# Cutting the first wq transfer by partitions: 16 rows, then 112 rows

## The chip, the cores and the metric

The kernel runs on one core of one Trainium2 chip. The metric is the device time of one execution in microseconds (us), lower is better. Beside timed runs there is one execution recorded by the hardware profiler; all places in time below count from the start of its span.

## What is computed

Two independent problems, A and B, of the same shape: one decoding step of sliding-window attention with grouped heads. Each takes two sequences of one token.

```python
def ref(x, k_cache, v_cache, wq, wo):          # x: [2, 1, 576]
    Hq, Dh, Hkv, Sk = 32, 128, 16, 16384
    W = 4096                                   # the window: the last 4096 positions
    q = (x @ wq).reshape(B, 1, Hq, Dh).transpose(0, 2, 1, 3)
    k = repeat(k_cache[:, :, Sk - W:, :], 2, axis=1)
    v = repeat(v_cache[:, :, Sk - W:, :], 2, axis=1)
    p = softmax(einsum("bhqd,bhkd->bhqk", q, k) * Dh ** -0.5)
    o = einsum("bhqk,bhkd->bhqd", p, v)
    return o.transpose(0, 2, 1, 3).reshape(B, 1, Hq * Dh) @ wo
out = concatenate([ref(A), ref(B)], axis=-1)   # bfloat16
```

All inputs are bfloat16. wq is 576 x 4096 (4608 KB), wo is 4096 x 576 (4608 KB), and the windows of K and V are 32 MB each for each problem.

## The kernel before

**Data.** Each problem's K and V are cut into slabs of 4 MB (one sequence, four K/V heads, 4096 positions), eight of K and eight of V for each problem. A slab fills one of four slots of `ring`, 128 partitions by 32,768 bytes. Ahead of the slabs the same memory holds wq: `ringf` is `ring` seen flat, and problem P's wq takes `QW` = 18,432 elements (36,864 bytes) of each partition from `P * QW` on. wq is read as one flat run of memory, cut into 128 equal rows, one for each partition. With 9 groups of 2048 columns in each row it is the right-hand side of the q matmuls.

**Order of the work.** A static list (`_Sched`) holds the operations of each engine in the order in which they were written; for each dependency between engines a semaphore wait is put in front of the operation. A DMA adds 16 to its semaphore when it has landed; `dma_op` takes the number of DMAs that one entry issues, so that a user waits for 16 times that number.

**The DMA queue.** SP issues all large transfers, in this order: wq of A, wq of B (L187), then the slabs (L378) with the parts of wo (L362) between them, and last the output (L658). The four x transfers, two rows each, are issued by ACT (L179). The two wq transfers and the first K slab (slot 3, which wq doesn't reach) wait for nothing. The second K slab goes into slot 0 and waits for the q matmuls of A (`first_deps`); the slabs for slots 1 and 2 wait for those of B. Every later slab waits for the last reader of its slot: the DVE transposes of a K slab (L433) or the PE matmuls of a V slab (L536). The last V slab and the last quarter of wo come in three pieces each (`v_cuts`, `w_cuts`).

**The start.** GpSimd makes constants and masks; DVE spreads and transposes x (L222, L229). PE then runs the q matmuls of A, nine groups of four (L279 for the first of each group, the helper line L264 for the others), as soon as wq of A has landed, and those of B when wq of B has. ACT evacuates q; two small PE steps and GpSimd bring it into the form `zq`.

**The loop.** For each of the 16 K slabs DVE transposes two halves into `xt` (L433), PE multiplies them with `zq` into scores (L459 and L264), and for every two slabs there is a maximum, an exponential on ACT (L497), a transpose on DVE (L506) and the sums. Three slabs later PE multiplies with V (L536), DVE reduces (L559, L566), and the result meets wo (L618, L639).

Of the kernel before, what the change touches and what calls it, by code (L numbers as in the profile page):

```python
# [62 lines left out]
def build_kernel(nc, probs, out):  # L63
# [25 lines left out]
    QW = NU * UW  # L89
# [3 lines left out]
    with es:  # L93
# [50 lines left out]
        ringf = ring[:].rearrange("p r f -> p (r f)")  # L144
# [16 lines left out]
        wq_sem = [sem("wq%d" % P) for P in range(NPROB)]  # L161
# [7 lines left out]
        def dma_op(eng, sem_h, n_dmas, fn, deps, tag):  # L169
            op = S.add(eng, fn, deps, tag)  # L170
            dma_count[sem_h] = dma_count.get(sem_h, 0) + 16 * n_dmas
            op.dma = (sem_h, dma_count[sem_h])
            return op
# [7 lines left out]
            x_dma.append(dma_op("act", x_sem[P], 2, f_x, [], "x%d" % P))  # L181

        wq_dma = {}
        for P in range(NPROB):
            def f_wq(e, P=P):
                src = probs[P][3].rearrange("a b -> (a b)").rearrange("(p f) -> p f", p=128)
                return e.dma_start(ringf[:, P * QW:(P + 1) * QW], src).then_inc(wq_sem[P], 16)  # L187
            wq_dma[P] = dma_op("sp", wq_sem[P], 1, f_wq, [], "wq%d" % P)

        pool = lambda fn, deps, tag: S.add("pool", fn, deps, tag)  # L190
        dve = lambda fn, deps, tag: S.add("dve", fn, deps, tag)
# [600 lines left out]
def bass_concat_heads__sliding_block_cached__sliding_block_cached__decode_kernel(  # L792
    nc, A_x, A_k_cache, A_v_cache, A_wq, A_wo, B_x, B_k_cache, B_v_cache, B_wq, B_wo, out,
):
    build_kernel(nc, [(A_x, A_k_cache, A_v_cache, A_wq, A_wo), (B_x, B_k_cache, B_v_cache, B_wq, B_wo)], out)
# [28 lines left out]
```

## Time and profile before

| | |
|---|---|
| median of 3 runs | 363.3 us (363.21 to 363.47) |
| span of the profiled execution | 361.8 us; its own time is not listed apart from it, the median is 1.5 us longer |
| busy: PE, DVE, ACT, POOL | 240.2, 218.7, 46.0, 24.3 us |
| DMA | 153.26 MB, mean 424 GB/s |
| wq of A: issue on SP, from issue to landing | at 0.80 us, 13.3 us |
| wq of B: issue on SP, from issue to landing | at 1.25 us, 23.8 us |

Busy time is the sum of an engine's instructions in the profiled execution. The time from issue to landing of a transfer holds its wait behind the transfers that were issued before it. The page cuts the span into 40 equal slices of some 9 us; its DMA row gives the mean busy share of the 16 DMA engines in tenths, and the GB/s row what they moved. A timeline row has the start, the duration, the engine, the line of the kernel, the operation with its output and inputs, and in brackets how long the engine had been idle and what released it.

### The profile page before, as it was taken

The numbers are of one execution on the slowest core, as the hardware profiler recorded it, in microseconds if no ns is written. First come the engines' busy times: TensorE is split into PE (matmuls) and PEld (weight loads), VectorE is DVE, ScalarE is ACT, GpSimd is POOL, SyncE is SP. The second block draws the span as 40 slices with busy tenths as digits, with TensorE's granted clock in tenths as the row PEclk, the third lists the DMA queues.
The fourth block names the chain that finished last, engine by engine and source line by source line (L and its number), as shares of the span: only waits on it lengthen the run. The fifth ranks groups of instructions, "written<-read, shape, count | busy, mean of one in ns | idle before, by whom it ended". The sixth has DMA issues, their size and how long they took to land.

```text
span 361.8 us, 2625 instructions
## 1 busy us (share of the span) xinstructions
PE 240.2 (66%) x1292; PEld 57.2 (16%) x927; DVE 218.7 (60%) x150; ACT 46.0 (13%) x78; POOL 24.3 (7%) x84
## 2 busy tenths in 40 slices
PE   0497787666485747662596675567776875668695
PEld 0000111112111201111121121112112121112222
DVE  1901898495929591934909585682927776674622
ACT  1002100040023000500005000500005000500500
POOL 4200101100010001000010000100010001000000
PEclk9999698969988996888788796888688796868969
DMA  8999999999999999999999999999999999999996
GB/s 327 457 435 406 460 408 446 424 431 438 417 453 408 457 404 428 444 431 431 435 420 444 417 449 410 440 431 438 424 442 412 449 417 429 435 435 431 417 412 256
DMA packets 6227, 153.26 MB, mean 424 GB/s; under 512 B 700, under 2 KB 840, under 8 KB 1224
## 3 DMA queue, kind: packets, MB, share of 16 engines
q1 hardware_dynamic: 6196, 153.10, 98.7%
q8 instruction: 8, 0.13, 0.1%
q14 instruction: 3, 0.02, 0.0%
q10 hardware_dynamic: 20, 0.01, 0.0%
HBM read 153.10 MB, written 0.00 MB: 423 GB/s over the span
## 4 chain that ended last, share of the span: by engine, by line
DMA 48%; DVE 26%; PE 16%; issue 8%; ACT 1%; POOL 0%; SPq 0%
DMA ring<-in_B_k_cache_dram 17%; DVE xt L433 16%; DMA ring<-in_A_k_cache_dram 13%; DMA ring<-in_B_v_cache_dram 9%; DMA ring<-in_B_wq_dram 7%; PE st L264 5%; PE st L459 5%; DMA wob<-in_B_wo_dram 3%; PE pj L264 2%; DVE oR L566 2%; DVE mx L467 2%; DVE pT L506 2%; DVE tmp L559 2%; PE ot L536 2%; PE pj L618 1%
## 5 line engine op out<-in xcount | busy, mean ns | idle before, releaser
L459 PE MATMUL st<-xt,zq 128*128 128x512 bf16 x256 | 124.1, 485 | 86.1 <-DVE xt L433 86.1
L433 DVE STREAM_TRANSPOSE xt<-ring 128x4096 f32<-128x4096 f32 x32 | 141.5, 4427 | 28.0 <-DMA ring<-in_A_k_cache_dram 18.8
L264 PE MATMUL st<-xt,zq 128*128 128x512 bf16 x256 | 122.7, 479 | 0.0
L497 ACT ACTIVATE pR<-st,bias 128x512 bf16<-128x512 f32 x32 | 40.0, 1414 | 222.9 <-DVE bias L490 222.9
L459 PEld LDWEIGHTS st<-xt,zq 128*128 128x128 bf16 x256 | 29.4, 115 | 210.1 <-issue 107.7
L536 PE MATMUL ot<-ring,pT 128*32 128x512 bf16 x512 | 32.6, 396 | 3.9 <-DMA ring<-in_B_v_cache_dram 3.9
L490 DVE SCALAR_TENSOR_TENSOR bias<-vmask,tb,offm 128x4 f32<-128x4 f32 x8 | 1.8, 223 | 43.0 <-PE tb L487 43.0
L520 DVE TENSOR_REDUCE ssum<-tb 128x2 f32<-128x8 f32 x8 | 1.3, 162 | 36.0 <-PE tb L517 36.0
L425 POOL TENSOR_TENSOR zq<-qs,bmask 128x64 bf16<-128x64 bf16 x32 | 8.7, 293 | 168.1 <-PE st L264 145.8
L506 DVE STREAM_TRANSPOSE pT<-pR 128x2048 bf16<-128x2048 bf16 x8 | 18.4, 2303 | 0.8 <-ACT pR L497 0.7
L279 PE MATMUL ot<-ring,pT 128*32 128x512 bf16 x18 | 7.6, 421 | 15.0 <-DMA ring<-in_A_wq_dram 14.2
L559 DVE SCALAR_TENSOR_TENSOR tmp<-ot,rsb,dmask 128x512 f32<-128x512 f32 x16 | 11.5, 719 | 7.9 <-PE ot L536 7.9
L566 DVE TENSOR_REDUCE oR<-tmp 128x128 f32<-128x512 f32 x15 | 15.6, 1042 | 0.5
L536 PEld LDWEIGHTS ot<-ring,pT 128*32 128x32 bf16 x512 | 12.4, 99 | 19.6 <-DMA ring<-in_B_v_cache_dram 5.5
L618 PE MATMUL pj<-wob,oM 128*2 128x288 bf16 x48 | 12.7, 299 | 0.0
L264 PE MATMUL pj<-wob,oM 128*2 128x288 bf16 x48 | 12.7, 299 | 0.0
L264 PE MATMUL pj<-ring,pT 128*32 128x512 bf16 x36 | 11.9, 416 | 0.0
L467 DVE TENSOR_REDUCE mx<-st 128x2 f32<-128x1024 f32 x8 | 9.7, 1213 | 0.1
L497 ACT ACTIVATION_READ_ACCUMULATOR pR<-st,bias 128x1 f32 x32 | 8.8, 276 | 0.0
L264 PE MATMUL st<-ring,pT 128*32 128x512 bf16 x18 | 7.3, 407 | 0.0
L222 DVE TENSOR_TENSOR xt<-xt,hmask 4x1152 bf16<-4x1152 bf16 x2 | 2.7, 1349 | 6.7 <-DMA xt<-in_A_x_dram 6.7
L469 POOL TENSOR_TENSOR mv<-mx,v 128x2 f32<-128x2 f32 x8 | 1.6, 195 | 75.8 <-DVE mx L467 75.8
(68 smaller groups left out, 75.6 us busy)
## 6 DMA issues: line engine op xcount, KB each, us to landing
ring<-in_A_k_cache_dram SPq DMA_DIRECT2D x8, 4096.0 KB, 24.3
ring<-in_A_v_cache_dram SPq DMA_DIRECT2D x8, 4096.0 KB, 29.9
ring<-in_B_k_cache_dram SPq DMA_DIRECT2D x8, 4096.0 KB, 27.0
ring<-in_B_v_cache_dram SPq DMA_DIRECT2D x7, 4096.0 KB, 29.8
ring<-in_A_wq_dram SPq DMA_DIRECT2D x1, 4608.0 KB, 13.3
ring<-in_B_wq_dram SPq DMA_DIRECT2D x1, 4608.0 KB, 23.8
wob<-in_A_wo_dram SPq DMA_DIRECT2D x2, 2304.0 KB, 28.3
wob<-in_B_wo_dram SPq DMA_DIRECT2D x1, 2304.0 KB, 27.4
```

Of the source, the lines that this page charges most:

```text
L264: return e.add_instruction(mybir.InstMatmult(name=nc.get_next_instruction_name(), engine=mybir.EngineType.PE, ins=[e.lower_ap(mv_), e.lowe ...
L279: last = e.matmul(QB[c], wt, mv_, start=first, stop=True, skip_group_check=True)
L425: last = e.tensor_tensor(dst, src, msk, ALU.mult)
L433: Xop[(t, jh)] = dve(lambda e: e.transpose(xt[:, jh, :].bitcast(FP32).rearrange("p (kp x kt) -> p x kp kt", kp=2, kt=2), ring[:, r, jh * H ...
L459: last = e.matmul(ob, wt, mv_, start=first, stop=True, skip_group_check=True)
L467: ch[(G, "max")] = dve(lambda e: e.tensor_reduce(mx[:], st[:, :].rearrange("p (x t) -> p t x", t=2), AX.X, ALU.max), [Sop[(2 * G + 1, 1)]] ...
L497: last = e.activation(pR[:].rearrange("p (x k) -> p k x", k=4)[:, kv, :], st[:, :].rearrange("p (x t) -> p t x", t=2)[:, kv % 2, :], ACTF.Exp,
L506: pT_op[G] = dve(lambda e: e.transpose(pT[:, v, :].rearrange("p (w j q) -> p j w q", w=4, q=8), pR[:].rearrange("p (j w q) -> p j w q", w= ...
L536: last = e.matmul(OTB[32 * c:32 * c + 32, :], pT[:, v, base + 32 * c:base + 32 * c + 32], ring[:, r, jj * 128:(jj + 4) * 128], start=rd == ...
L559: evac_op[i] = dve(lambda e: e.scalar_tensor_tensor(tv, o, rsb[:, v, b:b + 1], dm, ALU.mult, ALU.mult), deps, "ev%d" % i)
L566: ch[(G, "red%d" % b)] = dve(lambda e: e.tensor_reduce(oR[:, b, :], tmp[:].rearrange("p (j d) -> p d j", j=4), AX.X, ALU.add), [evac_op[i] ...
L618: last = e.matmul(PJ[h], oM[:, j, :], mv_, start=start and j == 0, stop=True, skip_group_check=True)
```

## The change

The transfer of A's wq is cut into two DMAs by partitions, both on SP's queue and both counted on the semaphore of A's wq: rows 0 to 15, then rows 16 to 127. B's wq stays one DMA. The q matmuls of A wait for both pieces.

```diff
         wq_dma = {}
+        q_cuts = [[0, 16, 128], [0, 128]]
         for P in range(NPROB):
             def f_wq(e, P=P):
                 src = probs[P][3].rearrange("a b -> (a b)").rearrange("(p f) -> p f", p=128)
-                return e.dma_start(ringf[:, P * QW:(P + 1) * QW], src).then_inc(wq_sem[P], 16)
-            wq_dma[P] = dma_op("sp", wq_sem[P], 1, f_wq, [], "wq%d" % P)
+                for p0, p1 in zip(q_cuts[P], q_cuts[P][1:]):
+                    last = e.dma_start(ringf[p0:p1, P * QW:(P + 1) * QW], src[p0:p1, :]).then_inc(wq_sem[P], 16)
+                return last
+            wq_dma[P] = dma_op("sp", wq_sem[P], len(q_cuts[P]) - 1, f_wq, [], "wq%d" % P)
```

## The prediction

> **What bounds the kernel now.** I read the slices and the queues of the page first, since they say whether an edit to one transfer can matter at all.
>
> ```profile
> DMA  8999999999999999999999999999999999999996
> GB/s 327 457 435 406 460 408 446 424 431 438 417 453 408 457 404 428 444 431 431 435 420 444 417 449 410 440 431 438 424 442 412 449 417 429 435 435 431 417 412 256
> ...
> q1 hardware_dynamic: 6196, 153.10, 98.7%
> ```
>
> Every slice but the first and the last is full on the DMA row, and SP's queue (q1, 153.10 MB) holds the 16 engines for 98.7% of the span. No compute engine comes near (PE 66%, DVE 60%). So the kernel is its transfers, one after the other, plus a head before the first byte and a tail behind the last.
>
> Then the timeline of the first 35 us, for when each transfer is issued and who waits for its landing.
>
> ```profile
> 0.80 0.39 SPq L187 DMA_DIRECT2D ring<-in_A_wq_dram  x1
> 1.25 0.41 SPq L187 DMA_DIRECT2D ring<-in_B_wq_dram  x1
> 1.71 32.52 SPq L378 DMA_DIRECT2D ring<-in_A_k_cache_dram  x4
> ...
> 14.20 0.61 PE L279 MATMUL ot<-ring,pT 128*32 128x512 bf16 x1 [14.20 <-DMA ring<-in_A_wq_dram]
> ...
> 25.07 0.39 PE L279 MATMUL ot<-ring,pT 128*32 128x512 bf16 x1 [0.79 <-DMA ring<-in_B_wq_dram]
> ...
> 34.77 8.77 DVE L433 STREAM_TRANSPOSE xt<-ring 128x4096 f32<-128x4096 f32 x2 [16.72 <-DMA ring<-in_A_k_cache_dram]
> ```
>
> The three first users show the landings: wq of A by 14.20, wq of B by 25.07, the first K by 34.77. B's 4,718,592 bytes took 25.07 - 14.20 = 10.87 us, 434 GB/s; K's 4,194,304 took 9.70 us, 432 GB/s. At 432 GB/s a transfer of 128 rows gives each engine eight rows of 36,864 bytes, 1.365 us each, and eight are 10.92 us. A's landing at 14.20 is therefore a head of some 3.3 us and then this rate.
>
> Last, windows of both ends (columns: window, length, five engines' busy time, granted clock, DMA share, GB/s).
>
> ```profile
> 1.70:5.00 3.30, 0.00 (x0) 0.00 (x0) 0.00 (x0) 1.28 (x1) 3.30 (x8) 1.00 1.01 358
> 5.00:14.20 9.20, 0.00 (x1) 0.01 (x1) 5.83 (x12) 0.00 (x0) 1.12 (x5) 1.00 1.04 450
> ...
> 357.00:358.00 1.00, 0.99 (x16) 0.49 (x12) 0.32 (x1) 0.00 (x0) 0.00 (x0) 1.00 0.78 311
> 358.00:359.00 1.00, 0.64 (x8) 0.29 (x8) 0.00 (x0) 0.00 (x0) 0.00 (x0) 1.00 0.56 213
> ```
>
> The start is a little slow (358 GB/s), and in the last two full microseconds the engines run dry at different times: 0.22 + 0.44 = 0.66 us of mean idle. The last wo piece lets its matmuls begin at 359.3, and the span ends at 361.8. The timed runs have a median of 363.3 us; I carry the 1.5 us between as a constant.
>
> **The change, part by part.** *Issue.* One more DMA start on SP ahead of everything else: 0.39 to 0.41 us by the two L187 rows, with a gap of 0.05. B's start moves from 1.25 to about 1.7 and K's from 1.71 to about 2.15. Neither waits for a semaphore, and A's rows keep the engines busy until about 14, so this is hidden: 0. Without that cover it would cost 0.45. No instruction gets a new wait; the first q matmul waits for both pieces, count 32 on the semaphore, where it waited for 16.
>
> *Head.* A start of sixteen rows is a shorter job than one of 128, so every engine may get its first row sooner. The bounds: no gain; or all of the 0.5 us from the end of the issue (1.19) to the first traffic (1.7) and the 0.57 us that 358 instead of 432 GB/s costs in a 3.3 us window, 1.1 together. The window after it runs at 450, so part of the 0.57 is bookkeeping between windows. I take 0.4, a gain.
>
> *Sixteen rows into sixteen partitions.* Before, all transfers of weight have 128 rows and write all 128 partitions; the trace has no large transfer into a few of them. The new piece has 16 x 36,864 = 589,824 bytes, and all 16 engines write partitions 0 to 15 at once. One end: the narrow target does not matter, 1.365 us, loss 0. The other: the sixteen rows go in one after the other, 16 x 1.365 = 21.8 us, loss 20.5. Between: the only rate the trace shows is 432 GB/s into 128 partitions, 3.38 GB/s each; sixteen at that rate take 54 GB/s, so 10.92 us instead of 1.365, loss 9.55. I take this, because it is the measured row scaled by what changes.
>
> [...]
>
> *The other 112 rows.* Seven rows for each engine, as many in all as before. Lower end 0: 7 x 1.365 = 9.55. Upper end by the same scaling, 112 of 128 partitions: 378 GB/s, 10.92 us, loss 1.37. I take 0, since 112 partitions are nearest to the row with 128, and keep 1.37 for the range.
>
> *Passing it on.* The DMA row has no idle slice and each engine serves SP's transfers in turn, so a loss at the front moves every later landing: wq of B, K, V, wo. It isn't made up by compute, which is not the bound. K's second transfer is issued at 24.31, on q's first half (L279), ten microseconds before the first K has landed; that margin moves along with the landings, so the queue does not run dry. Only the uneven ends give something back: a loss that differs between engines can fall partly into the 0.66 us of idle at the end. I take all of it.
>
> Sum: 9.55 + 0 - 0.4 - 0.66 + 0 = 8.5 us. Span 361.8 + 8.5 = 370.3, and with the 1.5 around it 371.8. This case runs from 368.3 (past half way to the next) to 363.3 + 9.55 + 1.37 = 374.2.
>
> **Rivals.**
> 1. *Not slower.* Sixteen partitions take in what sixteen engines send, and only the head counts: 363.3 - 0.4 = 362.9, at best 362.2. For it: the engines' own rate, 27 GB/s each, could be the limit rather than their target, and the slow 1.70:5.00 window is there to be gained. Against it: nothing in the trace has ever put 432 GB/s into so few partitions. It decides if the piece takes under 1.365 + 0.4 = 1.77 us, that is above 335 GB/s.
> 2. *Half the price.* The sixteen rows go in four at a time: 4 x 1.365 = 5.46 us, loss 4.1, the 112 rows free, all engines equally late so that nothing is absorbed: 363.3 + 4.1 - 0.4 = 367.0, from 365 to 368.3.
> 3. *The second piece collides too.* If its rows are dealt so that sixteen neighbours are written at a time, there are eight rounds like the first, each losing at least 4.1 us: 8 x 4.1 = 33 us, about 396. For it: nothing shows how 112 rows are dealt. Against it: 128 rows are dealt so that the full rate comes out.
> 4. *Not what it says.* The sixteen rows do not reach sixteen engines; one engine that takes them all ends 20.5 us late: some 383.
>
> **How the numbers follow.** Forecast 0.45, rival 1 0.20, rival 2 0.22, rival 3 0.09, rival 4 0.04. A measurement of this kernel can tell about 0.2% (0.73 us) from no change. Rival 1 is within that for 0.15 and faster by more for 0.05, where the head gains more than 0.73 of its 1.1; all others are slower, 0.80. The range leaves out rivals 3 and 4 and the best end of rival 1: 362.5 to 374.2, with about 0.86 in it. I predict 371.8 us.
>
> **What would show it.** In the changed profile: two L187 issues for A's wq ahead of B's; the first slices of GB/s far below 327 and 457; the first q matmul (14.20) near 22 to 23, the second half (25.07) and the first transpose (34.77) late by the same amount, and nothing lost after that: later slices as now. The interval between the first two landings should stay near 10.9 us. A shift of about 3.7 us at 14.20 is rival 2; a shift of 30 is rival 3. If 14.20 comes at 14.6 or sooner, the narrow piece is free and the forecast wrong. If the shift at the front is there but the end does not move, the step on passing it on is wrong.

## The result, and the profile after

The changed kernel takes 374.23 us (median of 5 runs, 373.85 to 374.73) against 363.24 before: 1.0304 times as long, 95% interval 1.0291 to 1.0316, or 11.0 us more. The forecast was 371.8 with a range up to 374.2: the direction was right, the size too small, and the measured time lies just outside the range. The profiled execution took 374.14 us with a span of 372.6, so the same 1.5 us lies around the span as was carried in the sum.

The slices and the main queue of the page after:

```profile
DMA  9999999999999999999999999999999999999995
GB/s 159 274 321 423 436 408 450 434 408 447 443 405 445 440 410 443 426 438 419 436 440 417 436 440 419 441 419 443 429 422 446 422 429 440 420 440 415 426 418 228
...
q1 hardware_dynamic: 6212, 153.10, 98.6%
```

The DMA row is as full as before. But in the first three slices the engines move 159, 274 and 321 GB/s where they moved 327, 457 and 435; from the fourth slice to the last but one the rates are of the size of before (405 to 450). A share of "9" stands beside 159 GB/s here as it stands beside 440: it does not show how fast the packets move.

The timeline after, with the rows that answer to those of before (the lines of the kernel have moved by three):

```profile
0.80 0.85 SPq L189 DMA_DIRECT2D ring<-in_A_wq_dram  x2
...
1.71 0.48 SPq L189 DMA_DIRECT2D ring<-in_B_wq_dram  x1
...
2.23 43.31 SPq L381 DMA_DIRECT2D ring<-in_A_k_cache_dram  x4
...
25.47 0.61 PE L282 MATMUL ot<-ring,pT 128*32 128x512 bf16 x1 [25.47 <-DMA ring<-in_A_wq_dram]
...
36.38 0.39 PE L282 MATMUL ot<-ring,pT 128*32 128x512 bf16 x1 [1.25 <-DMA ring<-in_B_wq_dram]
46.08 4.45 DVE L436 STREAM_TRANSPOSE xt<-ring 128x4096 f32<-128x4096 f32 x1 [22.64 <-DMA ring<-in_A_k_cache_dram]
```

The first q matmul comes at 25.47 instead of 14.20 (11.27 late, where the forecast had 22 to 23), B's at 36.38 instead of 25.07 (11.31), the first K transpose at 46.08 instead of 34.77 (11.31). Between A's and B's landing lie 10.91 us, between B's and K's 9.70, as before. The whole loss is made in A's wq, and everything behind it is late by that amount.

The line's own view has the time from issue to landing for the three transfers issued there, shortest, median and longest:

```profile
DMA to landing us min/median/max: 7.7/24.2/34.6
```

The shortest is the piece of sixteen rows: issued at 0.80, landed at 8.5. Before, wq of A landed 13.3 us after its issue, 2.4 of them more than its eight rows of 1.365 us; with the same 2.4 and one row, the piece would have landed at 0.8 + 2.4 + 1.4 = 4.6. So some 3.9 us are lost in the first piece, and 11.3 - 3.9 = 7.4 in the second. That split is the opposite of the forecast's, and the experiments are there to explain it. (The 4.6 is an estimate from the row of the kernel before; the experiments below give 2.7 to 3.9 for the first piece.)

### The profile page after: what moved, and what is told of

The parts are those of the page before. It is cut to its first block, busy times and chain, and to the rows that moved or that the text cites. A ratio compares the mean times of both kernels' runs of the same rounds, so it can differ in the third digit from the quotient of the medians.

```text
span 372.6 us, 2626 instructions
## 1 busy us (share of the span) xinstructions
PE 231.8 (62%) x1292; PEld 55.9 (15%) x927; DVE 218.3 (59%) x150; ACT 46.0 (12%) x78; POOL 23.3 (6%) x84
## 4 chain that ended last, share of the span: by engine, by line
DMA 40%; DVE 32%; PE 17%; issue 8%; ACT 1%; POOL 1%; SPq 0%; DVEq 0%
DVE xt L436 21%; DMA ring<-in_B_k_cache_dram 17%; DMA ring<-in_A_k_cache_dram 12%; DMA ring<-in_B_v_cache_dram 9%; PE st L462 7%; PE st L267 6%; DMA wob<-in_B_wo_dram 3%; DVE oR L569 3%; DVE pT L509 2%; DVE mx L470 2%; DVE tmp L562 2%; ACT pR L500 1%; PE pj L621 1%; PE pj L267 1%; PE ot L539 1%
## 5 line engine op out<-in xcount | busy, mean ns | idle before, releaser
L462 PE MATMUL st<-xt,zq 128*128 128x512 bf16 x256 | 120.1, 469 | 91.1 <-DVE xt L436 91.1
L267 PE MATMUL st<-xt,zq 128*128 128x512 bf16 x256 | 118.8, 464 | 0.0
L462 PEld LDWEIGHTS st<-xt,zq 128*128 128x128 bf16 x256 | 28.5, 111 | 210.1 <-DVE xt L436 107.5
L539 PE MATMUL ot<-ring,pT 128*32 128x512 bf16 x512 | 31.6, 386 | 7.4 <-DMA ring<-in_B_v_cache_dram 7.4
L282 PE MATMUL ot<-ring,pT 128*32 128x512 bf16 x18 | 7.4, 410 | 26.7 <-DMA ring<-in_A_wq_dram 25.5
L523 DVE TENSOR_REDUCE ssum<-tb 128x2 f32<-128x8 f32 x8 | 1.3, 163 | 32.3 <-PE tb L520 32.3
L539 PEld LDWEIGHTS ot<-ring,pT 128*32 128x32 bf16 x512 | 12.2, 97 | 22.4 <-DMA ring<-in_B_v_cache_dram 10.1
L282 PEld LDWEIGHTS ot<-ring,pT 128*32 128x32 bf16 x18 | 1.9, 103 | 41.3 <-DMA ring<-in_A_wq_dram 25.5
```

Of the source, the lines that this page charges most:

```text
L267: return e.add_instruction(mybir.InstMatmult(name=nc.get_next_instruction_name(), engine=mybir.EngineType.PE, ins=[e.lower_ap(mv_), e.lowe ...
L282: last = e.matmul(QB[c], wt, mv_, start=first, stop=True, skip_group_check=True)
L462: last = e.matmul(ob, wt, mv_, start=first, stop=True, skip_group_check=True)
L539: last = e.matmul(OTB[32 * c:32 * c + 32, :], pT[:, v, base + 32 * c:base + 32 * c + 32], ring[:, r, jj * 128:(jj + 4) * 128], start=rd == ...
```

## The experiments

All of them change only how A's wq is transferred. Theory T: the loss comes from which partitions are written at the same time. Theory S: from which rows of memory are read at the same time. Theory C: from the cut itself. One expectation speaks of "ways in": a way in stands for whatever neighbouring partitions might share when the engines write them. That is the author's picture; the runs show times and rates alone.

**Target or source.** Four kernels with eight DMAs of sixteen rows each; targets and sources are each either sixteen neighbours or sixteen that lie eight apart. In the four edits `w` is A's part of `ringf`, `src` its 128 rows:

```diff
 e1  (w[16*j:16*j+16, :], src[16*j:16*j+16, :])  for j in range(8)
 e2  (w[16*j:16*j+16, :], src[j:128:8, :])       for j in range(8)
 e3  (w[j:128:8, :],      src[16*j:16*j+16, :])  for j in range(8)
 e4  (w[j:128:8, :],      src[j:128:8, :])       for j in range(8)
```

Near target, near source. 

> A's wq in eight DMAs of sixteen neighbouring rows (16j to 16j+15), each into the same sixteen neighbouring partitions. Theory T (the loss comes from sixteen engines writing into sixteen neighbouring partitions): every one of the eight is like the first piece of the change, which landed at 8.5 us instead of some 4.6, so 8 x 3.9 = 31 us: 394 us. Theory S (the loss comes from reading sixteen neighbouring rows of wq at once): the same 394. Theory C (any further cut of a transfer costs, wherever its rows lie): eight cuts against one, far over the 11 us of the change. This run only sets the scale for the next three.

Near target, far source. 

> Eight DMAs, each into sixteen neighbouring partitions (16j to 16j+15) but from rows j, j+8, j+16 and so on of wq, so that the sixteen rows read at once lie 295 KB apart. The rows of wq stand permuted in SBUF, which changes the output and no shape. T: as e1_near_near, some 394 us. S: the loss is gone, about 363 us.

Far target, near source. 

> Eight DMAs, each from sixteen neighbouring rows of wq (16j to 16j+15) into partitions j, j+8, j+16 and so on to j+120. The rows of wq stand permuted in SBUF, which changes the output and no shape. S: as e1_near_near, some 394 us. T: the targets are spread, so far less. [...]

Far target, far source. 

> Eight DMAs of rows and partitions j, j+8 and so on to j+120, nothing permuted. [...] S: 363 us. If e3 and e4 agree and e1 and e2 agree, the source does not matter.

Measured: 392.48, 391.94, 374.70 and 374.97 us, against 363.21 for the kernel before on the same chip (ratios 1.0805 [1.0774, 1.0837], 1.0791 [1.0759, 1.0822], 1.0316 [1.0286, 1.0346], 1.0323 [1.0293, 1.0353]). With the source changed the time moves by 0.5 and 0.3 us, with the target changed by 17 to 18. Theory S falls. The windows of e1, inside its wq transfers (last column GB/s):

```profile
10.00:15.00 5.00, 0.00 (x0) 0.00 (x0) 4.19 (x11) 0.00 (x0) 1.15 (x5) 1.00 1.03 118
15.00:20.00 5.00, 0.00 (x0) 0.00 (x0) 0.87 (x1) 0.00 (x0) 0.00 (x0) 1.00 1.02 118
```

and of e3:

```profile
5.00:10.00 5.00, 0.00 (x0) 0.00 (x0) 3.34 (x4) 0.00 (x0) 0.26 (x1) 1.00 0.73 148
10.00:15.00 5.00, 0.00 (x0) 0.00 (x0) 4.91 (x11) 0.00 (x0) 2.27 (x5) 1.00 1.11 236
15.00:20.00 5.00, 0.00 (x0) 0.00 (x0) 1.38 (x3) 0.00 (x0) 0.00 (x0) 1.00 1.15 236
```

These windows have to be read with care. A row's bytes are booked where the row starts, and the rows start in rounds of sixteen, so a window of 5 us shows whole rounds: 118 GB/s is one round of sixteen rows (16 x 36,864 bytes in 5 us), 236 is two. In e3 two rounds do not fit into every 5 us; the window before has 148, and the three together have 207. A safer rate comes from the landing, which the first q matmul shows, in e1 and in e3:

```profile
43.67 0.61 PE L282 MATMUL ot<-ring,pT 128*32 128x512 bf16 x1 [43.67 <-DMA ring<-in_A_wq_dram]
...
26.11 0.61 PE L282 MATMUL ot<-ring,pT 128*32 128x512 bf16 x1 [26.11 <-DMA ring<-in_A_wq_dram]
```

In the kernel before it started at 14.20, after a transfer of 10.92 us at full rate. So A's wq takes 10.92 + 29.47 = 40.4 us in e1, 117 GB/s, and 22.8 us in e3, 207 GB/s. Sixteen neighbouring partitions take in 117 GB/s, sixteen that lie eight apart 207, all 128 in one DMA 432. The same number of partitions at two rates: it is not their number alone that counts, as the forecast's scaling to 54 GB/s had it, but where they lie. Why it counts, no run shows.

e4 shows one thing more. It brings the same rows into the same partitions as the kernel before, and is 11.8 us slower. So it matters which partitions are written together; and one DMA of 128 rows cannot well be dealt as e4 is, with rows eight apart at the same time (that cutting into more DMAs does not explain the loss, e8 below shows). How it is dealt, the profile does not show.

**The cut alone.** The same bytes in the first piece, but cut by columns:

```diff
 e5  [(w[:, 0:2304], src[:, 0:2304]), (w[:, 2304:QW], src[:, 2304:QW])]
```

> A's wq in two DMAs of the same bytes as in the change (an eighth, then seven eighths), but cut by columns: both have all 128 partitions. Theory T (neighbouring partitions share ways in; a transfer over all 128 is dealt so that it reaches all of them): the loss is gone, 363.2 us, within 0.5. Theory C (a second DMA in front costs by itself): some or all of the 11 us stay, up to 374.

Measured: 363.29 us against 363.26, ratio 1.0001, interval 0.9991 to 1.0010. A second DMA in front costs nothing that can be measured, and gains nothing. Theory C falls, as far as both pieces keep all 128 partitions.

**How the 112 rows are dealt.** The sevens written out by hand:

```diff
 e8  [(w[0:16, :], src[0:16, :])] + [(w[16+i:128:7, :], src[16+i:128:7, :]) for i in range(7)]
```

> Rows 0 to 15 first as in the change; the other 112 rows not as one DMA but as seven of sixteen rows, 16+i, 23+i, 30+i and so on, so that the engines are given by hand the rows they would get if one DMA of 112 rows were dealt in consecutive sevens. If it is dealt so: the time of the change, 374.2 us, within 1. If 112 rows are dealt in another way: something else; sixteen neighbours at a time would have been e1_near_near's 392.5, and is already ruled out by the change's own time. If the 112 rows cost nothing and the whole loss lay in the first sixteen (the prediction's split of it), this would also be 374 only by chance, since then the spread sevens cost nothing either: 363.2 + 3.6 (the first piece at the 118 GB/s of e1) = 367.

Measured: 373.62 us (ratio 1.0287, interval 1.0266 to 1.0307), within 0.6 of the change. The windows give more than the total. The changed kernel:

```profile
5.00:10.00 5.00, 0.00 (x0) 0.00 (x0) 1.82 (x2) 0.00 (x0) 0.27 (x1) 1.00 1.10 229
10.00:15.00 5.00, 0.00 (x0) 0.00 (x0) 3.69 (x10) 0.00 (x0) 1.15 (x5) 1.00 0.83 236
15.00:20.00 5.00, 0.00 (x0) 0.00 (x0) 0.73 (x1) 0.00 (x0) 0.00 (x0) 1.00 0.98 244
20.00:25.00 5.00, 0.00 (x0) 0.00 (x0) 3.36 (x5) 0.00 (x0) 0.00 (x0) 1.00 1.06 332
```

and with sevens by hand:

```profile
5.00:10.00 5.00, 0.00 (x0) 0.00 (x0) 1.90 (x2) 0.00 (x0) 0.26 (x1) 1.00 1.13 237
10.00:15.00 5.00, 0.00 (x0) 0.00 (x0) 4.93 (x11) 0.00 (x0) 1.83 (x4) 1.00 0.84 236
15.00:20.00 5.00, 0.00 (x0) 0.00 (x0) 2.79 (x5) 0.00 (x0) 0.44 (x2) 1.00 0.95 236
20.00:25.00 5.00, 0.00 (x0) 0.00 (x0) 0.00 (x0) 0.00 (x0) 0.00 (x0) 1.00 1.07 332
```

The windows agree, with the same rise in the last one, where the first rows of B's wq come in. By landings, 112 rows take 25.47 - 8.5 = 17.0 us, 243 GB/s.

The packed trace also has each row by itself, with its start and duration. Taken in rounds of sixteen by their starts, the seven rounds behind the first last 3.05, 2.52, 1.92, 2.21, 2.29, 2.48 and 2.37 us in the mean for the one DMA of 112 rows, and 3.08, 2.47, 1.94, 2.26, 2.28, 2.45 and 2.36 for the sevens by hand, where a row at full rate lasts 1.36. The one DMA of 112 rows thus behaves as if each engine got seven consecutive rows; the profile does not name an engine's rows, so this rests on the equal rounds and times. In the third of these rounds of the changed kernel fourteen rows last 1.70 to 2.00 us and two last 2.55 and 2.62. So a DMA of fewer than 128 rows doesn't slow every row to half; but no run here has sixteen rows of such a DMA at the full rate, so it is not shown that spreading them better would take away the whole loss.

**Each piece by itself.** An extra DMA of rows of 24,576 bytes into a place unused at that time, with wq left whole:

```diff
 e9   [(ringf[0:16, 2*QW:3*SW],   src[0:16, 0:3*SW-2*QW]),   (w, src)]
 e10  [(ringf[16:128, 2*QW:3*SW], src[16:128, 0:3*SW-2*QW]), (w, src)]
```

Sixteen rows. 

> wq as before in one DMA of 128 rows, and ahead of it an extra DMA of sixteen rows of 24,576 bytes into partitions 0 to 15 of a place that is not used until later: work added, none removed. It measures the first piece alone, at two thirds of its size. At full rate the extra 393,216 bytes cost 0.91 us: 364.1. At the 118 GB/s of e1_near_near 3.33 us: 366.5. At the prediction's 54 GB/s 7.3 us: 370.5.

112 rows. 

> wq as before in one DMA of 128 rows, and ahead of it an extra DMA of 112 rows of 24,576 bytes into partitions 16 to 127 of a place that is not used until later. It measures the second piece alone, at two thirds of its size. If 112 rows run at full rate (the prediction's step), 2,752,512 bytes at 432 GB/s cost 6.4 us: 369.6. By 112 of 128 partitions, 7.3 us: 370.5. If the 7.7 us that the change leaves after the first piece (11.3 - 3.6) are lost here, 6.4 + 2/3 x 7.7 = 11.5 us: 374.7.

Measured: 365.94 us (ratio 1.0075, interval 1.0055 to 1.0095) and 374.20 (1.0303, 1.0281 to 1.0324), against 363.26. The sixteen rows cost 2.7 us, 1.8 more than their bytes at full rate (0.91); at the change's size that is 1.5 x 1.8 = 2.7. This is less than the 3.3 us that 118 GB/s gave for the whole transfer of sixteen rows. The 112 rows cost 10.9, 4.5 more than their 6.4 at full rate; 1.5 x 4.5 = 6.8 at the change's size. Together 9.5 of the change's 11.0. The larger part is in the 112 rows by this way of measuring too.

**Fours, and the other order.**

```diff
 e7  [(w[0:64, :], src[0:64, :]), (w[64:128, :], src[64:128, :])]
 e6  [(w[16:128, :], src[16:128, :]), (w[0:16, :], src[0:16, :])]
```

Two halves. 

> A's wq in two DMAs of 64 rows, partitions 0 to 63 and 64 to 127. [...] If only a narrow piece like sixteen rows costs: 363 to 364. If an uneven number of rows (seven) were what costs in the 112 rows, fours would be free: 363.

112 rows first. 

> The two pieces of the change in the other order, 112 rows first. T: the same collisions in each piece, so the time of the change, 374.2, within 1. If the loss came from the first piece holding up the start (the second one's rows meeting engines out of step), it would shrink: the 112 rows start evenly, and only the sixteen at the end cost 3.6: 367.

Measured: 375.16 us (ratio 1.0328, interval 1.0298 to 1.0358) and 374.37 (1.0306, 1.0276 to 1.0336), against 363.21. Halves run at the rate of e3 (236 GB/s in a window, 207 by its landing), as a window and the landing show:

```profile
15.00:20.00 5.00, 0.00 (x0) 0.00 (x0) 2.37 (x3) 0.00 (x0) 0.19 (x1) 1.00 1.15 236
...
26.31 0.61 PE L282 MATMUL ot<-ring,pT 128*32 128x512 bf16 x1 [26.31 <-DMA ring<-in_A_wq_dram]
```

By the landing that is 23.0 us for A's wq, 205 GB/s; at the 236 of the window it would be 20.0 us, 3 us too low. So it is neither the odd seven nor a narrow piece alone that costs: two wide halves lose 11.95 us where the change loses 11.0. The order makes no difference that can be measured (374.37 against 374.23). In the swapped kernel the last sixteen rows can be seen holding up what comes behind them:

```profile
10.00:15.00 5.00, 0.00 (x0) 0.00 (x0) 3.10 (x4) 0.00 (x0) 0.00 (x0) 1.00 1.01 236
15.00:20.00 5.00, 0.00 (x0) 0.00 (x0) 2.41 (x8) 0.00 (x0) 1.15 (x5) 1.00 1.40 236
20.00:25.00 5.00, 0.00 (x0) 0.00 (x0) 4.08 (x5) 0.00 (x0) 0.00 (x0) 1.00 0.55 118
```

By 20.00 all 128 rows of A have started, the sixteen among them (from the start of the span to there the kernel moves 236 GB/s, which is 128 rows). In the next 5 us only sixteen rows start, the first of B's: the engines still hold the sixteen, which last 4.47 us each in the mean.

**Two further cuts.**

```diff
 e11  [(w[0:32, :], src[0:32, :]), (w[32:128, :], src[32:128, :])]
 e12  [(w[a:b, :], src[a:b, :]) for a, b in ((0, 48), (48, 80), (80, 128))]
```

Twos and sixes. 

> A's wq in 32 and 96 rows, one DMA each, so that the engines get consecutive twos and sixes. [...]

Threes, twos and threes. 

> A's wq in 48, 32 and 48 rows, so that the engines get threes, twos and threes. [...]

Measured: 374.03 us (ratio 1.0293, interval 1.0249 to 1.0338) and 384.20 (1.0573, 1.0528 to 1.0619), against 363.37: 10.7 and 20.8 us more. The first is 1.1 us below the halves, the second 9.0 above them. A window inside e12's last piece, and e12's landing:

```profile
25.00:30.00 5.00, 0.00 (x0) 0.00 (x0) 3.40 (x4) 0.00 (x0) 0.00 (x0) 1.00 0.98 125
...
35.61 0.61 PE L282 MATMUL ot<-ring,pT 128*32 128x512 bf16 x1 [35.61 <-DMA ring<-in_A_wq_dram]
```

By the landing A's wq takes 10.92 + 21.41 = 32.3 us in e12, 146 GB/s. Row by row the trace has, once a piece is under way, 2.7 to 2.9 us in the halves, 4.5 to 4.7 in e12's pieces of 48 rows and 5.05 to 5.09 in e1, against 1.36 at full rate. By landings the 112 rows of the change move 243 GB/s, the 96 rows of e11 some 220 (from 9.4 to 25.35 us), the halves 205 and the eight DMAs of e1 117. Why the pieces of 48 rows are so much slower than those of 64, no run shows.

None of these kernels is faster than the one before.

## Why the prediction was right and wrong

*What bounds the kernel, and passing it on: right.* 11.27 us at the first q matmul are 11.31 at the first K transpose and 10.8 at the end of the span. About 0.5 came back, where 0.66 was taken. That the uneven ends gave it is not shown: the first of the last three groups of matmuls with wo (356.84 before, 367.64 after) is already only 10.80 late.

*Issue: right.* B's and K's issues moved to 1.71 and 2.23, and e5 with the same number of DMAs costs nothing.

*Head: wrong, 0.4 too good.* Sixteen rows do not start sooner than 128. The windows of the changed kernel around the first traffic:

```profile
1.60:1.70 0.10, 0.00 (x0) 0.00 (x0) 0.00 (x0) 0.00 (x0) 0.10 (x1) 1.00 0.00 0
1.70:1.80 0.10, 0.00 (x0) 0.00 (x0) 0.00 (x0) 0.00 (x0) 0.10 (x1) 1.00 0.15 12
1.80:1.90 0.10, 0.00 (x0) 0.00 (x0) 0.00 (x0) 0.00 (x0) 0.10 (x2) 1.00 13.25 1843
```

The kernel before has the same in 1.80:1.90, and nothing of that size earlier:

```profile
1.80:1.90 0.10, 0.00 (x0) 0.00 (x0) 0.00 (x0) 0.00 (x0) 0.10 (x2) 1.00 6.25 1843
```

Between these two kernels the start does not change with the number of rows in the first DMA (16 and 128).

*Sixteen rows into sixteen partitions: a loss as forecast, but 9.55 is far too much.* Scaling with the number of partitions was the wrong measure, as e1 and e3 show with one number of partitions at two rates (117 and 207 GB/s). By landings it is 3.9, by the extra DMA 2.7, by 118 GB/s 3.6.

*The other 112 rows: the step that failed.* The forecast took 0 and at most 1.37, because 112 of 128 partitions looked nearest to a full transfer. It is 6.8 to 7.4 us. The bound of 1.37 was drawn from the same scaling with the number of partitions. What the runs show instead is that it counts which partitions the engines write at the same moment (sixteen neighbours or sixteen that lie eight apart): the 112 rows move 243 GB/s, and only pieces with all 128 partitions moved 432. The two errors ran against each other, 9.55 + 0 against some 3.9 + 7.4. That the total came within 2.4 us, and that the top of the range (374.2) came so close to the 374.23 measured, is luck: that top holds 9.55 + 1.37, and neither part is near its measured size.

*The rivals.* Rival 1 (only the head counts, some 362.9) and rival 4 (one engine takes all sixteen rows, some 383) fall with the time itself. Rival 2 (four at a time) had the price of the first piece nearly right, 4.1 against 2.7 to 3.9, and the second piece wrong. That four go in at a time no run shows: in the trace after, all sixteen rows of the first piece start between 1.82 and 2.95 us and last 3.90 to 4.76 us each. Rival 3 (the second piece collides too) was right that the second piece loses, 6.8 to 7.4 us, but took a worse dealing; that dealing is e1, which takes 392.5.

## What to carry to other kernels

In a kernel that is bound by its transfers, as this one is, a cut by partitions can cost time although no byte is added: before cutting, ask which partitions the engines will write at the same moment in each piece. Here a cut by columns, which keeps all 128 partitions in every piece, was free (363.29 us against 363.26), and every cut by partitions that was tried cost 10 us or more (10.4 to 29.3) on a transfer of 11. In the profile here the loss hides behind a full DMA row, a "9" at 159 GB/s as at 440; read the GB/s row beside it.

## What was not expected of the hardware

Two halves move 205 GB/s, the 112 rows 243 and e11's 96 rows some 220, where 128 rows in one DMA move 432. In the third round of the 112 rows two rows of sixteen were slow (2.55 and 2.62 us) and the others not quite at full rate (1.70 to 2.00 against 1.36). In other rounds the rows are all equally slow: all sixteen last 4.58 to 4.63 us in a round of e12's threes. Whether and how one engine's wait reaches the others was not tried and stays open, as does why the rows of e1 (5.05 us) last little longer than those of e12's threes (4.6).
